# VectorE's 128x1 products in the row chain: tensor_scalar in place of tensor_tensor

## The chip, the cores and the metric

The kernel runs on one core of one Trainium2 chip. The metric is the device time of one execution in microseconds (us). A core has TensorE (PE; its weight loads run beside the matmuls and are listed as PEld), VectorE (DVE), ScalarE (ACT), GpSimd (POOL), and SyncE (SP), which issues all of this kernel's DMAs.

## What is computed

The reference has two stages. Linear attention runs over 8 batches of 8 heads, 576 positions and 64 channels; its output, laid out as 4608 rows of 512, feeds a feed-forward block with a softmax-weighted activation and a layer norm.

```python
q_s = softmax(q, axis=-1)                # over the 64 channels
k_s = softmax(k, axis=2)                 # over the 576 positions
kv = einsum('bhsd,bhse->bhde', k_s, v)
x = einsum('bhsd,bhde->bhse', q_s, kv)   # as 4608 rows of 512
h = x @ w_in                             # 512 -> 1024
sm = softmax(h, axis=-1)
solu = h * sm
ln = (solu - mean(solu)) / sqrt(var(solu) + 1e-06) * g_ln
out = ln @ w_out                         # 1024 -> 512
```

## The kernel before

The 4608 rows are cut into 36 row tiles of 128 rows. A row tile passes through three pieces of work, each a Python generator that is advanced one step at a time: `attend` (or `attend_whole`) makes the transposed rows, `hidden` (for most later tiles behind `hidden_twin`, which makes the products of two tiles together) makes `h` in PSUM and carries it to the normalized `u`, and `project` multiplies `u` with `w_out`, scales the result and stores it. Other generators prepare the keys (`keys`, names `K`), the queries (`queries`, names `Q` and `R`) and the weights.

The order of all steps is written out by hand in the string `ORDER`. `h17` is one step of the chain of row tile 17, `o17` one of its projection, `x17` of its attention; `h17.v` is the same step with VectorE put in for the step's usual engine, if the step asks for its engine by `on(...)`. Each engine's queue holds its instructions in this order and executes them in it. An instruction that waits holds up those behind it.

The part around the change is the row chain in `hidden`, from the row maximum to `u`:

- ScalarE makes `nm`, the negated scaled maximum, and `e = exp(h * hs + nm)` with its sum `z` (L779);
- `am`, `pi` and `p = 1/pi` follow, three small 128x1 instructions; `p` is on GpSimd in every tile (L789);
- `ph = p * hs` (L792), on GpSimd by default, on VectorE where `ORDER` has `.v` for that step;
- VectorE multiplies `h` by `ph` and `e` in place (L795), ScalarE makes the mean `nmu` and the high half of `u` (L800), VectorE the low half (L802), and ScalarE the squares (L809). L809 is the last to read `h`: it sets free one of the two PSUM tiles called `h` that the matmuls of later row tiles (L765, or L697 for twins) write to;
- `z1`, `z2`, `var` (L813, L816, L819) and `r` (L822) are 128x1 instructions again. The first three are on VectorE or GpSimd as `ORDER` says.

`project` begins with `rr = r * osc` (L830), on GpSimd in every tile, and ends with the scaled copy of the product (L850 on ScalarE, L848 on VectorE).

VectorE's 128x1 instructions before are of two forms. `am`, `pi`, `z1`, `z2` and `var` are `tensor_scalar`: one input tensor and one or two scalar operands, of which one may be a 128x1 column. `ph` is `tensor_tensor`, with two input tensors.

Of the kernel before, what the change touches and what calls it, by code (L numbers as in the profile page):

```python
# [14 lines left out]
ALU = mybir.AluOpType  # L15
# [68 lines left out]
def linear_attention_solu_ffn(ctx: ExitStack, tc: tile.TileContext, q, k, v, w_in, w_out, g_ln, out):  # L84
# [7 lines left out]
    nc = tc.nc  # L92
# [25 lines left out]
    osc = cst.tile([P, 1], F32, name="osc")  # L118
# [21 lines left out]
    def on(default):  # L140

        return chosen["engine"] or default

    def cast(eng, out, x):
        if eng is nc.scalar:
            eng.copy(out, x)  # L146
        else:
            eng.tensor_copy(out, x)

    def cast_scaled(eng, out, x, scale):  # L150
        if eng is nc.scalar:
            eng.activation(out, x, AF.Copy, scale=scale)
        else:
            eng.tensor_scalar(out, x, scale, None, op0=ALU.mult)
# [38 lines left out]
    def load_v(b, i):  # L193

        if b > 0:
            nc.sync.dma_start(out=vm[:, i, :, 0:D], in_=heads_on_halves(v, b)[:, i].rearrange("p (c d) -> p c d", c=KC))
            return
        t = first_v[:, i]
        nc.sync.dma_start(out=t.rearrange("p c d -> p (c d)"), in_=heads_on_halves(v, b)[:, i])
        yield  # L200
        cast(on(nc.scalar), vm[:, i, :, 0:D], t)
# [160 lines left out]
    def tops_of(top, b):  # L362

        flat = top.rearrange("p n d -> p (n d)")
        if b >= ON_VECTOR:
            n = NP * D // 32
            blocks = sb.tile([P, n, 32], F32, name=f"blocks{b}", tag="kb", bufs=1)
            nc.vector.transpose(blocks.rearrange("p g r -> p (g r)"), flat)
            yield
            part = sm.tile([P, n], F32, name=f"part{b}", tag="part", bufs=2)  # L370
            nc.vector.tensor_reduce(part, blocks, axis=AX.X, op=ALU.max)
            yield
            swap = sm.tile([P, n], F32, name=f"swap{b}", tag="swap", bufs=2)
            for i in range(4):
                j = i ^ 1
                cast(on(nc.scalar), swap[32 * i : 32 * (i + 1)], part[32 * j : 32 * (j + 1)])
            yield
            nc.vector.tensor_tensor(part, part, swap, op=ALU.max)
            yield
            cols = sm.tile([P, n, 32], F32, name=f"cols{b}", tag="cols", bufs=1)  # L380
            cast(on(nc.scalar), cols, part.unsqueeze(2).broadcast_to([P, n, 32]))
            yield
            kb = sb.tile([P, NP, D], F32, name=f"kb{b}", tag="kb", bufs=1)
            nc.vector.transpose(kb.rearrange("p n d -> p (n d)"), cols.rearrange("p g r -> p (g r)"))
            yield kb
            return
# [193 lines left out]
    xT_of, uT_of, r_of, hs_of = {}, {}, {}, {}  # L580
# [159 lines left out]
    def hidden(row_tile):  # L740
# [10 lines left out]
        if row_tile in done:  # L751
            hs, minus = hs_of[row_tile[0]][:, 0:1], hs_of[row_tile[0]][:, 1:2]
        elif row_tile in whole:
# [5 lines left out]
            hs = one  # L759
        else:  # L760
# [9 lines left out]
            hs = hs_of[("rest", row_tile[0] // 2) if row_tile[1] == C else row_tile[0]][:, 0:1]  # L770
# [17 lines left out]
        p = sm.tile([P, 1], F32, name=f"p{name}", tag="p")  # L788
        nc.gpsimd.tensor_tensor(p, pi, mone, op=ALU.pow)  # L789
        yield  # L790
        ph = sm.tile([P, 1], F32, name=f"ph{name}", tag="ph")
        on(nc.gpsimd).tensor_tensor(ph, p, hs, op=ALU.mult)  # L792
        yield
        s1 = sm.tile([P, 1], F32, name=f"s1{name}", tag="s1")
        nc.vector.scalar_tensor_tensor(h, h, ph, e, op0=ALU.mult, op1=ALU.mult, accum_out=s1)  # L795
# [31 lines left out]
    def project(row_tile):  # L827
        uT, name, t = uT_of[row_tile], name_of(row_tile), tiles.index(row_tile)
        rr = sm.tile([P, 1], F32, name=f"rr{name}", tag="rr")
        nc.gpsimd.tensor_tensor(rr, r_of[row_tile], osc, op=ALU.mult)  # L830
        yield

        cuts = [slice(0, DM)] if t + 1 < len(tiles) else [slice(0, DM // 2), slice(DM // 2, DM)]
        for i, cols in enumerate(cuts):
            w = cols.stop - cols.start
            o_tag = "att" if t >= LATE and (t + i) % 2 else "o"
            o = ps.tile([P, w], F32, name=f"o{name}{i}", tag=o_tag, bufs=3 if o_tag == "att" else 1)
            for f in range(NF):
                for j, s in ((0, 0), (0, 1), (1, 0)):
                    nc.tensor.matmul(  # L840
                        o, uT[:, j, f], wo[:, s, f, cols], start=(f == 0 and j == 0 and s == 0), stop=(f == NF - 1 and j == 1)
                    )
                if f % 2 == 1:
                    yield
            part = sb.tile([P, w], F32, name=f"os{name}{i}", tag="os", bufs=2)
            eng = on(nc.scalar)
            if eng is nc.vector:
                eng.tensor_scalar(part, o, rr, None, op0=ALU.mult)  # L848
            else:
                eng.activation(part, o, AF.Copy, scale=rr)  # L850
            yield
            for rows, dst in destinations(row_tile):
                nc.sync.dma_start(out=dst[:, cols], in_=part[rows])
            yield

    def destinations(row_tile):
        b, c = row_tile
        if c < C:
            return [(slice(0, P), out[b * S : b * S + SM, :].rearrange("(p c) m -> p c m", c=C)[:, c])]
        return [(slice(j * R, (j + 1) * R), out[(b - 1 + j) * S + SM : (b + j) * S, :]) for j in range(2)]  # L860


    def name_of(row_tile):
        return f"{row_tile[0]}_{row_tile[1]}"
# [39 lines left out]
    for t, row_tile in enumerate(tiles):  # L904
        works[f"h{t}"] = hidden(row_tile)
        works[f"o{t}"] = project(row_tile)
# [59 lines left out]
```

## Time and profile before

| what | us |
|---|---|
| median of 3 runs (lowest to highest) | 453.46 (453.12 to 453.46) |
| the profiled execution's own time | 453.33 |
| its span, first to last instruction | 451.4 |
| TensorE busy in the span | 425.3 |
| VectorE busy | 361.5 |
| ScalarE busy | 298.8 |
| GpSimd busy | 261.1 |

The durations in the rows below are those of the profiled execution. Its time is 1.93 us above its span, so a span that is shorter by some microseconds is read as a time shorter by as much. The TensorE clock was granted at 0.999 of full speed over the span.

### The profile page before, as it was taken

Reading aid. Unit: us, or ns where it says so; the run is one execution under the profiler, and the core shown is the slowest. Engines: PE = TensorE matmul, PEld = TensorE weight load, DVE = VectorE, ACT = ScalarE, POOL = GpSimd, SP = SyncE. Lnnn points to the kernel's source line nnn. Section 1 sums busy time; section 2 is a strip of 40 time slices with the busy share of each in tenths; the row PEclk is TensorE's granted clock in tenths of the full one; section 3 lists DMA queues with packets and bytes.
Section 4 is the critical chain, followed back from the end, with each engine's and each line's share of the span. In section 5 each row is a group of like instructions: output and inputs, shape, how many; then the busy total and the mean of one; then the engine's idle time right before and its main releaser. Section 6 shows DMA issues by size and latency. Waiting matters only on the chain.

```text
span 451.4 us, 8807 instructions
## 1 busy us (share of the span) xinstructions
PE 425.3 (94%) x3297; PEld 203.3 (45%) x3297; DVE 361.5 (80%) x710; ACT 298.8 (66%) x529; POOL 261.1 (58%) x361
## 2 busy tenths in 40 slices
PE   0898899999999999998999999999899999999996
PEld 0443344454445444543544445444454444444444
DVE  5999999998999999888989898988888684653400
ACT  3889998685776978675785777593767671642511
POOL 4107885887987979747766895546576551140210
PEclk9999999999999999999999999999999999999999
DMA  8997689698796987886895669885462744344431
GB/s 274 401 323 275 125 187 188 153 222 180 170 189 171 179 206 164 206 194 145 173 220 119 120 163 212 176 200 113 97 141 49 154 94 103 71 81 94 57 115 50
DMA packets 167082, 73.98 MB, mean 164 GB/s; under 512 B 146424, under 2 KB 155904, under 8 KB 167040
## 3 DMA queue, kind: packets, MB, share of 16 engines
q1 hardware_dynamic: 167040, 73.42, 69.2%
q8 instruction: 26, 0.43, 0.4%
q14 instruction: 16, 0.13, 0.1%
HBM read 36.70 MB, written 9.44 MB: 102 GB/s over the span
## 4 chain that ended last, share of the span: by engine, by line
PE 67%; DVE 14%; ACT 6%; POOL 5%; DMA 4%; issue 4%; SPq 0%; ACTq 0%; DVEq 0%; POOLq 0%
PE o L840 33%; PE h L697 17%; PE h L765 10%; PE x L629 2%; PE kv L438 2%; DVE u L802 2%; DVE h L795 2%; DMA w_out<-in_moe_w_out_dram 2%; DVE ph L792 2%; DVE qnmx L488 1%; DMA qr<-in_q_dram 1%; POOL qm L490 1%; ACT qm L492 1%; POOL qhl L515 1%; DMA qm<-in_q_dram 1%
## 5 line engine op out<-in xcount | busy, mean ns | idle before, releaser
L840 PE MATMUL o<-wo,uT 128*128 128x512 f16 (+1 forms) x888 | 194.2, 373 | 0.5 <-ACT os L850 0.5
L840 PEld LDWEIGHTS <-uT 128*128 128x128 f16 x888 | 86.0, 98 | 98.6 <-issue 2.4
L765 PE MATMUL h<-wi,xT 128*128 128x512 f16 x336 | 75.8, 379 | 4.3 <-ACT e L809 4.3
L802 DVE SCALAR_TENSOR_TENSOR u<-h,nmu,u 128x1024 f16<-128x1024 f32 x36 | 45.9, 1278 | 13.5 <-ACT u L800 13.4
L765 PEld LDWEIGHTS <-xT 128*128 128x128 f16 x336 | 32.4, 98 | 44.0 <-issue 5.7
L795 DVE SCALAR_TENSOR_TENSOR h<-h,ph,e 128x1024 f32<-128x1024 f32 x36 | 46.3, 1288 | 7.3 <-POOL ph L792 3.6
L850 ACT ACTIVATE os<-o,rr 128x512 f32<-128x512 f32 (+1 forms) x31 | 21.0, 676 | 39.5 <-PE o L840 32.3
L809 ACT ACTIVATE e<-h,nmu 128x1024 f32<-128x1024 f32 x36 | 40.0, 1114 | 9.9 <-DVE u L802 9.6
L800 ACT ACTIVATE u<-h,nmu 128x1024 f16<-128x1024 f32 x36 | 40.0, 1112 | 1.1 <-ACT nmu L797 0.2
L697 PE MATMUL h<-wt,split 128*128 128x512 f16 x162 | 37.9, 379 | 0.0
L515 POOL TENSOR_TENSOR qhl<-qm,qhl 128x512 f16<-128x512 f32 x26 | 30.5, 1193 | 12.7 <-ACT qhl L146 12.2
L424 POOL TENSOR_TENSOR km<-km,kb 128x1152 f32<-128x1152 f32 x13 | 34.5, 2662 | 4.8 <-issue 3.6
L789 POOL TENSOR_TENSOR p<-pi,mone 128x1 f32<-128x1 f32 x36 | 22.8, 634 | 24.5 <-DVE pi L786 22.7
L490 POOL TENSOR_TENSOR qm<-qm,qnmx 128x1024 f32<-128x1024 f32 (+1 forms) x16 | 30.0, 1882 | 11.8 <-DVE qnmx L488 11.6
L779 ACT ACTIVATE e<-h,nm,hs 128x1024 f32<-128x1024 f32 x28 | 33.6, 1202 | 0.6
L697 PEld LDWEIGHTS <-split 128*128 128x128 f16 x216 | 21.0, 98 | 25.9 <-issue 1.2
L783 POOL TENSOR_SCALAR am<-nm 128x1 f32<-128x1 f32 x22 | 10.4, 471 | 38.4 <-ACT nm L775 38.1
L757 PE MATMUL h<-iw,xT 128*128 128x512 f32 x64 | 29.8, 601 | 2.4 <-ACT e L809 2.3
L508 POOL TENSOR_TENSOR qm<-qm,qrec 128x1024 f32<-128x1024 f32 x13 | 25.7, 1977 | 9.2 <-DVE qrec L499 8.9
L773 DVE TENSOR_REDUCE top<-h 128x1 f32<-128x1024 f32 x18 | 21.9, 1217 | 10.0 <-PE h L765 10.0
L822 POOL TENSOR_TENSOR r<-var,mhalf 128x1 f32<-128x1 f32 x36 | 21.2, 592 | 13.3 <-DVE var L819 12.4
L775 ACT ACTIVATE nm<-top,hs 128x1 f32<-128x1 f32 x28 | 8.2, 294 | 28.7 <-DVE top L733 20.2
(191 smaller groups left out, 729.8 us busy)
## 6 DMA issues: line engine op xcount, KB each, us to landing
km<-in_k_dram SPq DMA_DIRECT2D x7, 1152.0 KB, 7.6
vm<-in_v_dram SPq DMA_DIRECT2D x28, 288.0 KB, 4.9
out_dram<-os SPq DMA_DIRECT2D x31, 256.0 KB, 2.9
qm<-in_q_dram SPq DMA_DIRECT2D x7, 1024.0 KB, 6.2
wo<-in_moe_w_in_dram SPq DMA_DIRECT2D x4, 512.0 KB, 8.6
w_in<-in_moe_w_in_dram SPq DMA_DIRECT2D x4, 512.0 KB, 9.4
wo<-in_moe_w_out_dram SPq DMA_DIRECT2D x4, 512.0 KB, 5.4
w_out<-in_moe_w_out_dram SPq DMA_DIRECT2D x4, 512.0 KB, 8.2
```

Source lines behind the costliest of these rows:

```text
L424: on(nc.gpsimd).tensor_tensor(km[:, ns], km[:, ns], wide, op=ALU.subtract)
L490: on(nc.gpsimd).tensor_tensor(x, x, wide(nmx), op=ALU.add)
L515: on(nc.gpsimd).tensor_tensor(lo, y, hi, op=ALU.subtract)
L697: nc.tensor.matmul(out, lefts[left](s, i), right_block(right, r, i), start=(n == 0), stop=(n + 1 == len(terms)))
L757: nc.tensor.matmul(h[:, ns], xT[:, kc], iw[kc][:, ns], start=(i == 0), stop=(i == NP - 1))
L765: nc.tensor.matmul(h[:, ns], xT[:, t, kc], wi[:, s, kc, ns], start=(i == 0), stop=(i == len(terms) - 1))
L779: nc.scalar.activation(e, h, AF.Exp, bias=nm, scale=hs, accum_out=z)
L795: nc.vector.scalar_tensor_tensor(h, h, ph, e, op0=ALU.mult, op1=ALU.mult, accum_out=s1)
L800: nc.scalar.activation(u[:, 0], h, AF.Identity, bias=nmu)
L802: nc.vector.scalar_tensor_tensor(u[:, 1], h, nmu, u[:, 0], op0=ALU.add, op1=ALU.subtract)
L809: nc.scalar.activation(e, h, AF.Square, bias=nmu, accum_out=s2)
L840: nc.tensor.matmul(o, uT[:, j, f], wo[:, s, f, cols], start=(f == 0 and j == 0 and s == 0), stop=(f == NF - 1 and j == 1))
```

## The change

A helper makes a product of two 128x1 columns: `tensor_scalar` with the second column as scalar operand where the engine is VectorE, `tensor_tensor` as before elsewhere. The two places that make such products call it. In the second place the engine is now asked for by `on(...)`, as in the first.

```diff
+    def product_of(eng, out, x, y):
+
+        if eng is nc.vector:
+            eng.tensor_scalar(out, x, y, None, op0=ALU.mult)
+        else:
+            eng.tensor_tensor(out, x, y, op=ALU.mult)
+
...
         ph = sm.tile([P, 1], F32, name=f"ph{name}", tag="ph")
-        on(nc.gpsimd).tensor_tensor(ph, p, hs, op=ALU.mult)
+        product_of(on(nc.gpsimd), ph, p, hs)
...
         rr = sm.tile([P, 1], F32, name=f"rr{name}", tag="rr")
-        nc.gpsimd.tensor_tensor(rr, r_of[row_tile], osc, op=ALU.mult)
+        product_of(on(nc.gpsimd), rr, r_of[row_tile], osc)
```

`ORDER` has `.v` at nine steps that make `ph`, and at no step that makes `rr`. So nine instructions of VectorE change their form; no instruction is added or taken out, and none changes its place in its engine's queue or its waits. One of the nine places in VectorE's queue, for row tile (3, 2), before (L792 is `ph`, L736 the row maximum of the twin tile, L795 the product in place):

```order
L736 ISA top_2_3_2662 128x1
L792 TENSOR_TENSOR ph_2_2782<-p_2_2754,hs_2069 128x1 [waits Pool_49]
L795 SCALAR_TENSOR_TENSOR h_2_2596,s_2_2784<-h_2_2596,ph_2_2782,e_2_2708 128x1024 [waits DVE_49,Activation_49]
L670 SCALAR_TENSOR_TENSOR sums_0_2771<-x_0_0_2723,xT_0_2770 128x256 [waits PE_49,Activation_49]
L802 SCALAR_TENSOR_TENSOR u_2_2789<-h_2_2596,nmu_2_2786,u_2_2789 128x1024 [waits DMAHW5_49,Activation_49]
```

The same place in the changed kernel, where the helper's seven lines shift the later line numbers and `ph` carries the helper's line:

```order
L743 ISA top_2_3_2662 128x1
L153 TENSOR_SCALAR ph_2_2782<-p_2_2754,hs_2069 128x1 [waits Pool_49]
L802 SCALAR_TENSOR_TENSOR h_2_2596,s_2_2784<-h_2_2596,ph_2_2782,e_2_2708 128x1024 [waits DVE_49,Activation_49]
L677 SCALAR_TENSOR_TENSOR sums_0_2771<-x_0_0_2723,xT_0_2770 128x256 [waits PE_49,Activation_49]
L809 SCALAR_TENSOR_TENSOR u_2_2789<-h_2_2596,nmu_2_2786,u_2_2789 128x1024 [waits DMAHW5_49,Activation_49]
```

Nothing moved: only the operation of `ph` is another, and the same instructions stand ahead of it and behind it.

## Rows read from the trace of the kernel before

**Rows 1.** The page's busy times: us, share of the span, instructions.

```profile
PE 425.3 (94%) x3297; PEld 203.3 (45%) x3297; DVE 361.5 (80%) x710; ACT 298.8 (66%) x529; POOL 261.1 (58%) x361
```

**Rows 2.** The stretches: busy time of each engine, clock, DMA share, GB/s.

```profile
105.00:150.00 45.00, 43.17 (x382) 20.47 (x381) 43.25 (x79) 30.74 (x56) 37.95 (x40) 1.00 0.83 175
150.00:200.00 50.00, 50.00 (x417) 23.94 (x416) 45.65 (x90) 39.30 (x71) 39.07 (x55) 1.00 0.86 190
220.00:305.00 85.00, 85.00 (x735) 40.85 (x734) 75.47 (x163) 61.74 (x114) 56.36 (x76) 1.00 0.80 172
320.00:430.00 110.00, 109.79 (x693) 50.93 (x692) 70.50 (x148) 60.27 (x107) 42.09 (x84) 1.00 0.47 98
```

**Rows 3.** Timeline of TensorE: start, duration, instructions, [idle before and releaser].

```profile
116.83 0.41 PE L629 MATMUL x<-qT,bd 64*64 64x256 f16 x6 [0.70 <-DVE bd L471]
...
126.99 3.61 PE L765 MATMUL h<-wi,xT 128*128 128x512 f16 x16 [0.77 <-ACT e L809]
...
146.53 3.83 PE L765 MATMUL h<-wi,xT 128*128 128x512 f16 x17 [0.35 <-ACT e L809]
...
215.24 5.34 PE L765 MATMUL h<-wi,xT 128*128 128x512 f16 x24 [1.82 <-ACT e L809]
...
319.71 2.53 PE L765 MATMUL h<-wi,xT 128*128 128x512 f16 x11 [1.37 <-ACT e L809]
```

**Rows 4.** Line 792 on VectorE: duration ns min/median/max, first and last start.

```profile
L792 DVE TENSOR_TENSOR ph<-p,hs x9: 147/1850/2576, 109.2 to 391.3; 128x1 f32<-128x1 f32 x9
```

**Rows 5.** The same instructions by line: busy us, mean ns | idle before, releaser.

```profile
L792 DVE TENSOR_TENSOR ph<-p,hs 128x1 f32<-128x1 f32 x9 | 11.4, 1264 | 1.5 <-POOL p L789 1.5
```

**Rows 6.** Timeline around the first three long `ph`, VectorE and GpSimd.

```profile
109.18 1.90 POOL L508 TENSOR_TENSOR qm<-qm,qrec 128x1024 f32<-128x1024 f32 x1
109.24 1.85 DVE L792 TENSOR_TENSOR ph<-p,hs 128x1 f32<-128x1 f32 x1 [0.44 <-POOL p L789]
...
111.19 1.29 DVE L795 SCALAR_TENSOR_TENSOR h<-h,ph,e 128x1024 f32<-128x1024 f32 x1
...
119.12 1.92 DVE L792 TENSOR_TENSOR ph<-p,hs 128x1 f32<-128x1 f32 x1
...
131.58 1.85 DVE L792 TENSOR_TENSOR ph<-p,hs 128x1 f32<-128x1 f32 x1 [0.45 <-POOL p L789]
```

**Rows 7.** Timeline around the fourth, with the chain down to `e`.

```profile
207.16 5.20 POOL L424 TENSOR_TENSOR km<-km,kb 128x1152 f32<-128x1152 f32 x2
207.22 2.57 DVE L792 TENSOR_TENSOR ph<-p,hs 128x1 f32<-128x1 f32 x1
...
209.90 1.29 DVE L795 SCALAR_TENSOR_TENSOR h<-h,ph,e 128x1024 f32<-128x1024 f32 x1
...
212.66 1.28 DVE L802 SCALAR_TENSOR_TENSOR u<-h,nmu,u 128x1024 f16<-128x1024 f32 x1 [1.14 <-ACT u L800]
...
213.98 1.11 ACT L809 ACTIVATE e<-h,nmu 128x1024 f32<-128x1024 f32 x1 [0.30 <-DVE u L802]
```

**Rows 8.** Timeline around the fifth.

```profile
311.61 2.63 POOL L424 TENSOR_TENSOR km<-km,kb 128x1152 f32<-128x1152 f32 x1
311.67 2.58 DVE L792 TENSOR_TENSOR ph<-p,hs 128x1 f32<-128x1 f32 x1 [0.33 <-POOL p L789]
```

**Rows 9.** VectorE's 128x1 tensor_scalar with a column as scalar: ns min/median/max.

```profile
L816 DVE TENSOR_SCALAR z<-z x16: 118/204/214, 75.8 to 430.1; 128x1 f32<-128x1 f32 x16
L819 DVE TENSOR_SCALAR var<-s,z x13: 195/209/215, 115.4 to 430.4; 128x1 f32<-128x1 f32 x13
```

**Rows 10.** Timeline: such a tensor_scalar inside a long GpSimd instruction.

```profile
127.03 1.90 POOL L490 TENSOR_TENSOR qm<-qm,qnmx 128x1024 f32<-128x1024 f32 x1 [0.48 <-DVE qnmx L488]
...
128.00 0.20 DVE L816 TENSOR_SCALAR z<-z 128x1 f32<-128x1 f32 x1
```

**Rows 11.** VectorE's 128x1024 tensor_scalar, from its line: ns min/median/max.

```profile
L251 DVE TENSOR_SCALAR gw<-gw x4: 630/689/1125, 35.8 to 49.3; 128x1024 int32<-128x1024 int32 x4
```

**Rows 12.** A wide VectorE tensor_tensor, from its line: ns min/median/max.

```profile
L413 DVE TENSOR_TENSOR khalf<-km x9: 684/1208/1869, 6.6 to 281.7; 128x1024 f32<-128x1024 f32 x7, 128x512 f32<-128x512 f32 x2
```

## The prediction, made before the changed kernel ran

> **What bounds the kernel now.** I read the page first, then the stretches, then TensorE's waits, then VectorE's instructions on the changed line. TensorE is busy 94% of the span, VectorE 80%, GpSimd 58% [rows 1]. The stretches say more than that share. From 105 us on, TensorE has almost no idle time: 1.83 us between 105 and 150, none between 150 and 200, none between 220 and 305, and 0.21 us between 320 and 430 [rows 2]. A microsecond taken off VectorE can therefore shorten the kernel only where TensorE stands still because VectorE is late.
>
> There are five such places behind the first long `ph` [rows 3]. TensorE is idle 0.70 us until 116.83 for `bd` of VectorE, and then 0.77, 0.35, 1.82 and 1.37 us, until 126.99, 146.53, 215.24 and 319.71, each time for `e` (L809). L809 is the last reader of a PSUM tile `h` that the next matmuls write to. It waits for VectorE's L802, that for `nmu`, that for the product L795, and L795 for `ph`. Together the five are 5.01 us. That is the most I can see for this change to win; the starts of the matmuls in between follow TensorE's own pace.
>
> **What a `ph` on VectorE costs now.** The nine take from 147 to 2576 ns, with a median of 1850 [rows 4], though each makes 128 numbers. The timeline says why. The first starts 0.06 us after GpSimd's L508 and ends at 111.09; L508 ends at 111.08 [rows 6]. The fourth starts 0.06 us after the first of two instructions of L424, which together take 5.20 us, and ends at 209.79, when half of that time is over [rows 7]. The fifth starts 0.06 us after another L424, which ends at 314.24; `ph` ends at 314.25 [rows 8]. So `ph` is not computing for these 2 us. It is held until GpSimd's instruction is through. It comes behind such an instruction easily, because it waits for `p`, which is GpSimd's, and GpSimd goes straight on to its next work. Five of the nine are held, for 1.85, 1.92, 1.85, 2.57 and 2.58 us [rows 6 to 8], together 10.77 us of the 11.4 us that the nine take [rows 5]. The other four share the rest, some 0.15 us each.
>
> **What it costs afterwards.** The trace has the new form already: 128x1 `tensor_scalar` with a 128x1 column as scalar, `z2` and `var`. Sixteen and thirteen of them run on VectorE, and the longest takes 215 ns, with medians of 204 and 209 [rows 9]. Among that many, with GpSimd busy for 58% of the span, some must meet a long GpSimd instruction, and one is shown: L816 starts at 128.00, 0.97 us into a L490 that runs to 128.93, and is done in 0.20 us [rows 10]. I take 0.205 us for each new `ph`. The bounds are 0.118 us, the shortest of rows 9, and 2.58 us, if it is held like the old one.
>
> [...]
>
> **The sum.** VectorE's time falls by 10.77 - 5 x 0.205 = 9.7 us at the five held places and rises by 4 x 0.05 = 0.2 us at the other four. Those four lie behind 220 us, the last at 391.3 [rows 4], where TensorE works without a pause and VectorE has idle time left [rows 2]; at 0.05 us each I cost them at nothing, and at 0.2 us if that cover is gone. The helper itself costs nothing on the chip, and `rr` stays where it was.
>
> What reaches TensorE, place by place:
>
> - Fourth `ph`: it ends 2.57 - 0.2 = 2.37 us sooner, at 207.4. L795, `nmu`, `u` and L802 follow each other with no other wait, so `e` ends at 213.98 + 1.11 - 2.37 = 212.7 [rows 7]. TensorE's work ahead of the gap ends at 215.24 - 1.82 = 213.4. The gap of 1.82 us closes, with 0.7 us to spare.
> - Fifth: 2.58 - 0.2 = 2.38 us sooner against a gap of 1.37 us. It closes, with 1.0 us to spare.
> - First three: 1.65, 1.72 and 1.65 us sooner, 5.0 us in all, against gaps of 0.70, 0.77 and 0.35 us. VectorE is busy for 43.25 of the 45 us there [rows 2], so what one `ph` gives is carried on to the next. The second and third gap should close: the `ph` right ahead of each gives more than the gap takes. The first hangs on `tensor_tensor` work of VectorE between `ph` and `bd` that is itself open to being held: VectorE will now come to it while L508 still runs, until 111.08. I count 0.20 of its 0.70 us.
>
> That is 1.82 + 1.37 + 0.77 + 0.35 + 0.20 = 4.5 us. Against the profiled execution's own 453.33 us it gives 448.8 us; that execution is 0.13 us below the median of the runs shown, which is within their spread. With the whole of the first gap it is 448.3. The late side next is TensorE itself: between 150 and 200 us and from 220 us on it works without a pause, and an earlier TensorE starts each later stretch earlier with VectorE, which is earlier by at least as much.
>
> **The rivals.** What can be told from no change here is about 0.2%, 0.9 us.
>
> Part of it is given back. After the first three places VectorE is busy 45.65 of 50 us, with the DMA engines at 0.86 [rows 2]; a TensorE that is 1.8 us earlier could find its data late there, and the first three gaps open again further on. Then only the fourth and fifth count: 453.33 - 3.19 = 450.1 us. Against it speaks that VectorE has gained 5.0 us by then and TensorE asks for 1.8.
>
> Nothing comes of it, in one of two ways. Either `tensor_scalar` is held as `tensor_tensor` was, against which rows 9 and 10 speak, or TensorE waits at the same five places for something that stands behind `ph` by chance, a DMA or GpSimd. Both give 453.3 us, within 0.9.
>
> It becomes slower. VectorE's other `tensor_tensor` instructions can be held too: those of L413 take 1208 ns in the median and 1869 once [rows 12], 0.66 more. If the shift brings VectorE to such an instruction just behind the start of a long GpSimd one, where it came just ahead before, it loses up to 2.6 us, the length of one L424 [rows 8]. It decides from the point where such new holds, at places where TensorE has no slack, add to more than the 4.5 us won plus 0.9: three of 2.6 us would give 453.33 - 4.5 + 7.8 = 456.6 us. For it speaks that the order is fixed by hand and the two engines meet anew everywhere behind 109 us. Against it speaks that a hold of 2 us costs TensorE at most 1.8 us even now, with VectorE not ahead.
>
> **How the numbers follow.** I give the forecast 0.56, the part given back 0.27, nothing 0.11 and slower 0.06. The time is 448.8 us. The likeliest case's own range is 448.0 to 449.6. The range for 8 in 10 begins at 447.9, where the five gaps are closed (448.3) and the run is lower by 0.4 us, about the 0.34 us by which the runs of before differ. It reaches to 451.4, past the 450.1 of the second case, to where only 1.9 of the 5.0 us are kept. It leaves out no change and slower, some 0.17, and little more. Faster by more than 0.2% has 0.84, within 0.2% 0.10, slower 0.06.
>
> **What the changed profile would show.** Right: nine `ph` on VectorE of some 0.2 us with no long one; the five waits of TensorE in rows 3 gone or moved; TensorE's busy time still 425 us in a span of some 447 us; VectorE's busy time down by about 9 us. Wrong step by step: a `ph` near 2 us says that the form is held too; short ones with the 1.82 and 1.37 us still there say that another wait stood behind; those gone and new idle time on TensorE between 130 and 305 us says that it was given back; L413, L415, L417 or L293 longer than before says where. A slower kernel would come from those lines.

## The result, and the profile after

The changed kernel takes 447.07 us in the median of four runs (447.0 to 447.38), against 453.35 us for the kernel before in the runs beside it (453.12 to 453.46). The ratio is 0.9863, with a 95% interval from 0.9846 to 0.9881. That is 6.28 us faster, where I had forecast 4.5. The time lies below my range, which began at 447.9. The mechanism was the one I described and none of the rivals came; what the closing of the five gaps is worth was too small in the sum.

The busy times on the page answer to [rows 1]:

```profile
PE 425.1 (96%) x3297; PEld 203.3 (46%) x3297; DVE 352.8 (79%) x710; ACT 299.4 (67%) x529; POOL 261.8 (59%) x361
```

TensorE does the same work in the same time, 425.1 us against 425.3, in a span of 445.1 us in place of 451.4. VectorE is busy 8.7 us less.

The new `ph` on VectorE by line, with the mean duration in ns, answers to [rows 5]:

```profile
L153 DVE TENSOR_SCALAR ph<-p,hs 128x1 f32<-128x1 f32 x9 | 1.9, 208 | 1.5 <-POOL p L796 1.5
```

Nine of them take 1.9 us in place of 11.4, and in the grouped view the shortest is 199 ns and the longest 215. The place of the first long one, VectorE and GpSimd, answers to [rows 6]:

```profile
109.04 1.90 POOL L515 TENSOR_TENSOR qm<-qm,qrec 128x1024 f32<-128x1024 f32 x1
109.11 0.21 DVE L153 TENSOR_SCALAR ph<-p,hs 128x1 f32<-128x1 f32 x1 [0.44 <-POOL p L796]
...
109.42 1.29 DVE L802 SCALAR_TENSOR_TENSOR h<-h,ph,e 128x1024 f32<-128x1024 f32 x1
...
110.76 0.46 DVE L424 TENSOR_TENSOR ktop<-khalf 128x256 f32<-128x256 f32 x1
```

`ph` begins 0.07 us after GpSimd's 1.90 us instruction, as before, and is through in 0.21 us, while GpSimd goes on. The product L802 starts at 109.42, where it started at 111.19. The `tensor_tensor` L424, which I feared would be held in its place, starts at 110.76, inside L515, which ends at 110.94, and takes 0.46 us. At the same place before, with no GpSimd instruction of that length beside it, it took 0.41: it is held for 0.05 us at most.

All waits of TensorE between 105 and 430 us (in total, times, longest, in us), where before [rows 3] showed five of up to 1.82 us:

```profile
PE h L704 <- DVE vw L734: 0.4, 2, 0.2
PE o L847 <- ACT os L857: 0.2, 1, 0.2
```

Both stood in the kernel before with the same times. Behind 430 us there is one more wait of 0.26 us for `os`, as before.

And the stretches, cut where the work of TensorE corresponds to that of [rows 2]:

```profile
105.00:147.50 42.50, 42.50 (x383) 20.37 (x382) 39.23 (x79) 31.57 (x57) 39.19 (x41) 1.00 0.88 189
147.50:197.30 49.80, 49.80 (x416) 23.86 (x415) 45.24 (x89) 38.73 (x69) 38.38 (x54) 1.00 0.86 186
197.30:215.30 18.00, 17.59 (x94) 7.87 (x93) 15.11 (x34) 12.43 (x25) 12.04 (x19) 1.00 0.87 199
215.30:300.30 85.00, 85.00 (x735) 40.83 (x734) 75.83 (x163) 61.76 (x114) 56.57 (x76) 1.00 0.80 171
300.30:313.70 13.40, 13.40 (x76) 6.04 (x74) 11.73 (x26) 7.60 (x15) 9.75 (x14) 1.00 0.49 102
313.70:423.70 110.00, 109.79 (x693) 50.99 (x692) 69.89 (x146) 59.54 (x106) 41.50 (x82) 1.00 0.44 97
```

The first column behind the stretch is its length, the second TensorE's busy time. They are equal almost throughout, and the 0.41 us between 197 and 215 us are waits that stood there before: no new idle time took the place of the old.

**Where the 6.3 us come from.** I follow the start of the same run of matmuls in both timelines of TensorE. The difference of the starts grows at the five places and stays as it is between them.

| run of matmuls | start before | start after | earlier by | gained at this place | idle shown before |
|---|---|---|---|---|---|
| `o`, ahead of the first gap | 112.59 | 112.46 | 0.13 | | |
| `o`, behind the first | 117.17 | 116.05 | 1.12 | 0.99 | 0.70 |
| `o`, behind the second | 133.18 | 130.98 | 2.20 | 1.08 | 0.77 |
| `h`, behind the third | 146.53 | 143.82 | 2.71 | 0.51 | 0.35 |
| `h`, behind the fourth | 215.24 | 210.52 | 4.72 | 2.01 | 1.82 |
| `h`, behind the fifth | 319.71 | 313.45 | 6.26 | 1.54 | 1.37 |

The five gaps gave 6.13 us, and showed only 5.01 us of idle time. At the fourth the rows say why. Before, from TensorE's timeline:

```profile
208.08 5.34 PE L840 MATMUL o<-wo,uT 128*128 128x512 f16 x24 [0.20 <-ACT os L850]
```

It is followed by the run at 215.24 with 1.82 us of idle time [rows 3]. After, the same two runs:

```profile
205.34 5.34 PE L847 MATMUL o<-wo,uT 128*128 128x512 f16 x24 [0.20 <-ACT os L857]
210.52 5.34 PE L772 MATMUL h<-wi,xT 128*128 128x512 f16 x24
```

A run of 24 matmuls is listed as 5.34 us, but when nothing is late the next run starts 5.18 us after it began. The listed end lies 0.16 us behind the point from which the next run could have started. From start to start it was 7.16 us before and is 5.18 us now: 1.98 us, for an idle time that shows as 1.82. The other gaps understate in the same way, by 0.16 to 0.3 us each. The remaining 0.13 us stood already ahead of the first changed instruction (the first `ph` starts at 109.11 after and at 109.24 before), so the change did not make them.

### The profile page after: what moved, and what is told of

Read it like the earlier page. It is cut to its first block, busy times and chain, and to the rows that moved or that the text cites. A ratio compares the mean times of both kernels' runs of the same rounds, so it can differ in the third digit from the quotient of the medians.

```text
span 445.1 us, 8807 instructions
## 1 busy us (share of the span) xinstructions
PE 425.1 (96%) x3297; PEld 203.3 (46%) x3297; DVE 352.8 (79%) x710; ACT 299.4 (67%) x529; POOL 261.8 (59%) x361
## 4 chain that ended last, share of the span: by engine, by line
PE 84%; ACT 4%; DVE 4%; DMA 3%; issue 2%; POOL 1%; SPq 0%; ACTq 0%; POOLq 0%; DVEq 0%
PE o L847 41%; PE h L704 18%; PE h L772 16%; PE x L636 3%; PE kv L445 3%; DMA w_in<-in_moe_w_in_dram 2%; DMA km<-in_k_dram 2%; PE h L764 1%; ACT km L433 1%; DVE h L802 1%; DVE iw L260 1%; POOL am L790 1%; ACT gw L256 0%; ACT wi L287 0%; DVE iw L258 0%
## 5 line engine op out<-in xcount | busy, mean ns | idle before, releaser
L802 DVE SCALAR_TENSOR_TENSOR h<-h,ph,e 128x1024 f32<-128x1024 f32 x36 | 46.3, 1288 | 7.2 <-POOL ph L155 3.6
L431 POOL TENSOR_TENSOR km<-km,kb 128x1152 f32<-128x1152 f32 x13 | 34.5, 2664 | 4.8 <-issue 3.6
L764 PE MATMUL h<-iw,xT 128*128 128x512 f32 x64 | 30.9, 620 | 2.4 <-ACT e L816 2.3
L790 POOL TENSOR_SCALAR am<-nm 128x1 f32<-128x1 f32 x22 | 9.4, 428 | 38.2 <-ACT nm L782 37.9
L515 POOL TENSOR_TENSOR qm<-qm,qrec 128x1024 f32<-128x1024 f32 x13 | 25.7, 1977 | 9.9 <-DVE qrec L506 9.6
```

The lines of the kernel that those rows point to most:

```text
L431: on(nc.gpsimd).tensor_tensor(km[:, ns], km[:, ns], wide, op=ALU.subtract)
L764: nc.tensor.matmul(h[:, ns], xT[:, kc], iw[kc][:, ns], start=(i == 0), stop=(i == NP - 1))
```

## The experiments

My theory: the hold of five `ph` behind GpSimd's long instructions is all that the change removes, each place gives its start-to-start time, and the four short ones give nothing. The rivals: the gain comes from some other shift (the four short ones, the new line's position, less VectorE time in general); or any instruction of VectorE with one input is free, whatever its width. The edits are shown against the changed kernel.

**The first three places alone, and the last two alone.** In each, the other places get the old form back:

```diff
-        product_of(on(nc.gpsimd), ph, p, hs)
+        eng = on(nc.gpsimd)
+        if eng is nc.vector and name not in ('1_2', '1_3', '2_0'):
+            eng.tensor_tensor(ph, p, hs, op=ALU.mult)
+        else:
+            product_of(eng, ph, p, hs)
```

The second has `('3_2', '5_2')` in place of the three names, the third the four that are not held, `('5_0', '6_0', '6_2', '7_1')`.

> The new form at the first three held places alone (row tiles (1, 2), (1, 3) and (2, 0)); the other six of VectorE keep tensor_tensor. Theory: what a closed gap gives is the delay of the next matmul's start, which is more than the idle time that the profile shows, because the shown end of the last matmul ahead of it is modelled late. By the starts in the traces of before and after the three give about 2.6 us: 450.7 us. Rival, idle as shown: 0.70 + 0.77 + 0.35 = 1.8 us, 451.5 us, and the rest of the 6.3 us comes from somewhere else. Rival, given back: the DVE-bound stretch behind 150 us takes it again, 453.3 us.

Measured: 450.79 us against 453.24, ratio 0.9945 (0.993 to 0.9961), 2.45 us faster. By the table the first three give 2.58 us from start to start, by the idle time shown 1.82. The waits of TensorE keep the other two places:

```profile
PE h L772 <- ACT e L820: 3.2, 2, 1.8
```

> The new form at the fourth and fifth held place alone (row tiles (3, 2) and (5, 2)). Theory: about 3.5 us by the starts in the two traces, 449.8 us, and together with the first three the whole 6.3 us of the change within 0.3. Rival, idle as shown: 1.82 + 1.37 = 3.2 us, 450.1 us, with 1 us missing in the sum of both.

Measured: 449.76 us, ratio 0.9925 (0.9911 to 0.9939), 3.48 us faster; the table says 3.55, the idle time shown 3.19. Here the other three gaps stay:

```profile
PE h L772 <- ACT e L820: 1.1, 2, 0.8
PE x L636 <- DVE bd L478: 0.7, 1, 0.7
```

The two halves make 5.93 us together, against 6.17 for the whole change, if its 447.07 is set beside the same 453.24. So the places add up within 0.24 us, less than the 0.39 us by which the runs of before differ here, and one does not spoil another. Both halves come nearer to the starts than to the idle time shown.

**The four short ones alone.**

> The new form at the four places that were not held (row tiles (5, 0), (6, 0), (6, 2), (7, 1)). Theory: 0.05 us longer each and hidden, 453.35 us within 0.2. Rival: the 1.1 to 1.8 us that the idle times do not explain come from these, 452 us.

Measured: 453.4 us, ratio 1.0002 (0.9994 to 1.0011): no change. These four take 201 to 214 ns in place of some 150. TensorE's waits list the same five gaps as before, 5.0 us in all, so nothing of it reaches TensorE, as costed.

**The whole product on GpSimd.** This removes the hold without the new form, since VectorE then has no `ph` at all:

```diff
-        product_of(on(nc.gpsimd), ph, p, hs)
+        nc.gpsimd.tensor_tensor(ph, p, hs, op=ALU.mult)
```

> All nine ph as tensor_tensor on GpSimd, so none on VectorE: the hold is avoided without the new form. Theory (what counts is that VectorE is not held behind the long GpSimd instruction): GpSimd makes ph in 0.19 us right behind p and starts its long instruction that much later; the five gaps close all the same, 447.1 us within 0.4. Rival, the form itself matters or GpSimd, which is 0.2 us later at each place, is on the path: 448 to 450 us.

Measured: 449.7 us, ratio 0.9924 (0.9911 to 0.9938). That is 3.54 us faster. It is not the number that my theory gave, and it lies in the range of the rival. GpSimd's timeline at the first and the fifth place shows what I had left out:

```profile
109.03 1.90 POOL L515 TENSOR_TENSOR qm<-qm,qrec 128x1024 f32<-128x1024 f32 x1
110.89 0.18 POOL L799 TENSOR_TENSOR ph<-p,hs 128x1 f32<-128x1 f32 x1
...
307.40 0.56 POOL L796 TENSOR_TENSOR p<-pi,mone 128x1 f32<-128x1 f32 x1
307.93 2.62 POOL L431 TENSOR_TENSOR km<-km,kb 128x1152 f32<-128x1152 f32 x1
310.52 0.18 POOL L799 TENSOR_TENSOR ph<-p,hs 128x1 f32<-128x1 f32 x1
```

The hand-written order has the long instruction between `p` and `ph` here. On VectorE, `ph` had to wait for it as a neighbour, 1.85 us at the first place [rows 6] and 2.58 at the fifth [rows 8]; on GpSimd it waits for it in the queue, and takes 0.18 us once it comes. TensorE's waits keep these two gaps:

```profile
PE h L772 <- ACT e L816: 1.4, 1, 1.4
PE x L636 <- DVE bd L478: 0.8, 1, 0.8
```

The other three are closed. They are worth 1.08 + 0.51 + 2.01 = 3.60 us by the table and 2.94 by the idle time shown; measured were 3.54. At those three places `ph` stands ahead of the long instruction in GpSimd's queue, and the gap closes without the new form, so neither reason that the rival gave is needed. The theory of the hold stands, and my expectation failed on the order in GpSimd's queue.

**The old and the new form beside each other.** The changed kernel gets a spare 128x1 instruction ahead of `ph` at the five places. Nobody reads its result. Once it has two input tensors, once one and a scalar column:

```diff
-        product_of(on(nc.gpsimd), ph, p, hs)
+        eng = on(nc.gpsimd)
+        if name in ('1_2', '1_3', '2_0', '3_2', '5_2'):
+            spare = cst.tile([P, 1], F32, name=f"spare{name}", tag="spare")
+            nc.vector.tensor_tensor(spare, p, p, op=ALU.mult)
+        product_of(eng, ph, p, hs)
```

The second has `nc.vector.tensor_scalar(spare, p, p, None, op0=ALU.mult)` in that line.

> The changed kernel with a spare 128x1 tensor_tensor (p times p, into a tile that nobody reads) right ahead of ph at the five held places; ph itself stays tensor_scalar. Theory, the hold comes with a second input tensor in SBUF while GpSimd runs, whatever reads the result: the spare is held for 1.8 to 2.6 us at each place, and the time goes back to 453.3 us within 0.5. Rival, ph was late for another reason, the arrival of p or hs: the spare waits for p alone and takes 0.15 us, 447.2 us.

Measured: 454.0 us, ratio 1.0018 (1.0008 to 1.0027). All that the change had won is gone, and 0.74 us more, 0.2 us beyond what I had allowed. The likely reason is that the spare and `ph` now stand one behind the other at each place; TensorE's waits at the five places are 5.4 us where they were 5.0. The five spares, in ns min/median/max:

```profile
L802 DVE TENSOR_TENSOR spare<-p x5: 1850/1918/2572, 109.1 to 312.0; 128x1 f32<-128x1 f32 x5
```

> The same spare as tensor_scalar with p as its scalar. Theory: 0.2 us at each of the five places, not held; VectorE has that to spare, 447.1 us within 0.4, which also repeats the changed kernel's time. Rival, one more VectorE instruction is enough to bring the gaps back: 448 us or more.

Measured: 447.31 us, ratio 0.9868 (0.9854 to 0.9883).

```profile
L802 DVE TENSOR_SCALAR spare<-p x5: 204/214/215, 109.2 to 307.1; 128x1 f32<-128x1 f32 x5
```

Same values, same place, same count of instructions: 1.9 to 2.6 us with two inputs, 0.2 us with one. The form is what matters, and an added instruction on VectorE at the tightest place costs almost nothing in the other form.

**How wide may it be?** The spare now takes a wider input, the first columns of a constant 128x128 tile, times `p` as scalar operand; at the fifth place it is a 128x1 copy.

```diff
-        product_of(on(nc.gpsimd), ph, p, hs)
+        eng = on(nc.gpsimd)
+        wide = {"1_2": 2, "1_3": 3, "2_0": 16, "3_2": 128, "5_2": 1}.get(name)
+        if wide:
+            spare = cst.tile([P, wide], F32, name=f"spare{name}", tag=f"spare{wide}")
+            if wide == 1:
+                nc.vector.tensor_copy(spare, p)
+            else:
+                nc.vector.tensor_scalar(spare, ident[:, 0:wide], p, None, op0=ALU.mult)
+        product_of(eng, ph, p, hs)
```

> The spare is now, from the first place to the fifth: tensor_scalar of 128x2, 128x3, 128x16 and 128x128 (a constant f32 tile times p), and a 128x1 copy of p. It asks from which width on tensor_scalar is held too. [...] Theory B, a narrow tensor_scalar is never held: every spare takes 0.1 to 0.3 us, 447.3 us.

Measured: 452.23 us in the one run, 4.9 us above the time that I had put down for theory B. Four gaps stay open and the fifth closes, which by the table alone leaves 451.7 us; the spares add to that, as in the run with two inputs. The timeline of VectorE at the five places, and GpSimd's instruction at the first, the second and the last:

```profile
108.90 1.90 POOL L515 TENSOR_TENSOR qm<-qm,qrec 128x1024 f32<-128x1024 f32 x1
108.96 1.86 DVE L806 TENSOR_SCALAR spare<-ident,p 128x2 f32<-128x2 f32 x1 [0.44 <-POOL p L796]
...
118.25 5.21 POOL L431 TENSOR_TENSOR km<-km,kb 128x1152 f32<-128x1152 f32 x2
118.97 1.93 DVE L806 TENSOR_SCALAR spare<-ident,p 128x3 f32<-128x3 f32 x1
...
131.56 1.87 DVE L806 TENSOR_SCALAR spare<-ident,p 128x16 f32<-128x16 f32 x1 [0.45 <-POOL p L796]
...
207.31 2.64 DVE L806 TENSOR_SCALAR spare<-ident,p 128x128 f32<-128x128 f32 x1
...
311.88 2.63 POOL L431 TENSOR_TENSOR km<-km,kb 128x1152 f32<-128x1152 f32 x1
311.95 0.15 DVE L804 COPY spare<-p 128x1 f32<-128x1 f32 x1 [0.33 <-POOL p L796]
```

From two columns on, `tensor_scalar` is held to the end of GpSimd's instruction just as `tensor_tensor` was, at three columns too (at the second and the fourth place the two L431 are listed as one, and the spare ends where the first is through); the single column goes through in 0.15 us with 2.56 us of GpSimd's instruction left. To see that the width decides and not the place, the widths are exchanged: 128, 128, 64, 2 and 16 columns at the five places.

> The same with the widths at other places: 128x128, 128x128, 128x64, 128x2 and 128x16 from the first place to the fifth, so that width and place can be told apart. [...] Theory B (none held): 0.1 to 0.3 us each, 447.3 us.

Measured: 454.48 us in the one run, 7.2 us above the time of theory B and 1.2 us above the kernel before in the runs beside it (453.26 us), of which 0.25 us lie ahead of the first gap (its `o` starts at 112.84, before at 112.59) and the rest was not followed up. All five are held:

```profile
L806 DVE TENSOR_SCALAR spare<-ident,p x5: 1883/1983/2596, 109.5 to 312.6; 128x128 f32<-128x128 f32 x2, 128x64 f32<-128x64 f32 x1, 128x2 f32<-128x2 f32 x1, 128x16 f32<-128x16 f32 x1
```

Two and 16 columns are now held at the fourth and fifth place, and the fifth place, free in the run before, is held too.

The wide spares read `ident` and the narrow ones `p`, so width and tile change together; a 128x1 spare that reads `ident` was not tried. The changed kernel's own timeline has a 128x16 `tensor_scalar` that reads another tile, `qsum`. It ends at 176.95, 0.03 us behind the end of GpSimd's instruction, and takes 0.51 us where the median of its line is 0.17:

```profile
176.25 0.67 POOL L522 TENSOR_TENSOR qhlr<-qr,qhlr 128x256 f16<-128x256 f32 x1
176.44 0.51 DVE L504 TENSOR_SCALAR qden<-qsum 128x16 f32<-128x16 f32 x1
```

All of these inputs lie in SBUF. Two 128x2 `tensor_scalar` of the kernel before read `kv`, which lies in PSUM, with a constant as scalar, and both are through in 0.22 us inside a GpSimd instruction that runs to 97.84:

```profile
95.94 1.90 POOL L490 TENSOR_TENSOR qm<-qm,qnmx 128x1024 f32<-128x1024 f32 x1
...
97.06 0.22 DVE L445 TENSOR_SCALAR den<-kv 128x2 f32<-128x2 f32 x2
```

## Why the prediction was right, and where it was too small

- **What bounds the kernel.** Right. The five gaps of [rows 3] were all that the nine `ph` held up: three of them closed, two of them closed, and all five closed move the time by amounts that add up.
- **What a `ph` costs now.** Right. The hold by GpSimd's instruction was read from the ends in [rows 6 to 8], and the spare of two inputs is held at the same five places for the same 1.85 to 2.57 us.
- **What it costs afterwards.** Right: 0.205 us assumed, 0.208 measured in the mean. The short instruction inside a long one of GpSimd, of which [rows 10] show one, was a fair sample: none of the nine is held. What spoke against the change, that `tensor_scalar` might be held too, is borne out as well, by the wider spares, which take 1.86 to 2.64 us, only not for one column (below).
- **The four short ones** cost nothing, as costed.
- **The sum.** This is the step that failed: "Together the five are 5.01 us. That is the most I can see for this change to win". The five were worth 6.13 us. Two terms are too small. I took the idle time that the view lists as the time that TensorE loses. It begins at the listed end of the last matmul, and that was later than the point from which a matmul that is ready would have started, by 0.16 us at the fourth gap; counted from start to start the same gaps are 0.99, 1.08, 0.51, 2.01 and 1.54 us. That makes up 1.1 us. The other term is the first gap, of which I counted 0.20 of 0.70 us because I expected a new hold of `tensor_tensor` work between `ph` and `bd`. VectorE reached that work only at 110.76, 0.18 us before GpSimd was through, so hardly anything was held; that makes up 0.5 us. The lower end of the range, 447.9 us, was worked out from the same 5.01 us, so it was too high by the first term. With both terms as measured the sum is 453.33 - 6.13 = 447.2 us, against 447.07.
- **The rivals.** Part given back: no, TensorE has no new idle time behind 105 us. Nothing comes of it: no. Slower by new holds: no hold of that size came. A small one did: a 128x16 `tensor_scalar` of L504 takes 509 ns once, where its longest was 191 before; TensorE did not wait for it.

Left open: about 0.2 us between the sum of the halves and the whole. The start of `o` ahead of the first gap, 0.13 us earlier in the changed kernel, is 0.03 and 0.04 us earlier in the halves, so it explains little of them. No version faster than the changed kernel was found: between 105 and 430 us TensorE waits for 0.6 us in all.

No run tried whether a VectorE instruction that comes first holds GpSimd in its turn, but the trace of the kernel before points to it, on the `ph` that run on GpSimd:

```profile
L792 POOL TENSOR_TENSOR ph<-p,hs x19: 189/189/842, 85.3 to 410.1; 128x1 f32<-128x1 f32 x19
91.52 1.35 DVE L424 TENSOR_TENSOR km<-km,kb 128x1152 f32<-128x1152 f32 x1
92.07 0.84 POOL L792 TENSOR_TENSOR ph<-p,hs 128x1 f32<-128x1 f32 x1
```

The longest starts 0.55 us into VectorE's `tensor_tensor` and ends at 92.91, 0.05 us behind it. Another, of 0.85 us at 150.34, ends 0.05 us behind VectorE's L413 in the same way.

## What to carry to other kernels

When a tiny VectorE instruction takes microseconds, compare its end with the end of the GpSimd instruction that runs beside it. At the first, the third and the fifth place here the two ends agreed to 0.01 us, and the instruction was held and not computing; a form with one input column and a scalar operand freed it, from 1.85 to 2.58 us down to 0.2, where it was one column wide. To size a gap on TensorE, compare the start-to-start time of its neighbours with that of the same pair where nothing is late, and do not take the listed idle time, which was too small by 0.16 to 0.3 us at each of five gaps here. Moving the small instruction to GpSimd avoided that hold but not the queue, where it stood behind an instruction of 1.90 and one of 2.62 us at two of the five places: look first at what stands ahead of it there, and at what VectorE runs beside it.

## What was not expected of the hardware

The step between one and two columns is sharp. With input and output in SBUF, a `tensor_scalar` or copy of 128x1 takes 0.15 to 0.21 us beside a running GpSimd instruction; a `tensor_scalar` of 128x2, 128x3, 128x16, 128x64 and 128x128 takes 1.86 to 2.64 us, as long as GpSimd's instruction has still to run. Three columns are held, for 1.93 us; one is not; and two columns read from PSUM are not, two such instructions being through in 0.22 us. What makes the step was not shown: in the spares, width and input tile changed together.
